# The output projection's moving operand read as two halves in turn

## The chip, the cores and the metric

The kernel runs on one core of one Trainium2 chip. The metric is the device time of one execution in microseconds, the median of the runs shown; lower is better. A run of the kernel before took 280.85 us in the median of three (279.88 to 282.11). Engines are named as the profile names them: PE (TensorE matmul), PEld (TensorE weight load), DVE (VectorE), ACT (ScalarE), POOL (GpSimd), SP (SyncE, which issues all DMAs here).

## The reference

Inputs are q, k and v of shape (8 batches, 8 heads, 576 positions, 64), three weights and a convolution kernel of five taps. Two stages follow each other:

```python
# attention inside chunks of 64 positions, per batch and head
scores = q_c @ k_c.T / 8;  attn = softmax(scores);  out = attn @ v_c
# x: (8, 576, 512), heads side by side
gate = sigmoid(sum over k of conv_w[k] * x shifted by k)      # causal, per batch
val  = x @ w_val                                              # 512 x 512
y    = (gate * val) @ w_out                                   # 512 x 512
```

The last line is the output projection: 4608 rows of 512 numbers times a 512x512 weight.

## The kernel before, in words

The 4608 rows are cut into nine groups g of 512. Attention of a group makes x transposed (features on the 128 partitions, 512 positions along the free dimension, four feature blocks), and the value product and the gate keep this layout. So the output projection of a group, `pr(g, t, c)`, takes as its stationary operand (`lhsT`, loaded by PEld) 128 positions t of the gated values of feature block c, and as its moving operand (`rhs`, streamed by PE) the 512 columns of feature block c of w_out. The result is 128 positions by 512 output features in one PSUM tile `ps`, accumulated over the four blocks c.

Both large products are made in three passes of a four-byte format (fp32r), from a high and a low part of each operand: high x high, high x low, low x high. `pr` issues three matmuls of 128x128 by 128x512; there are 9 x 4 x 4 pieces `P g t c`, so 432 such matmuls. The value product `va` (pieces `V g m c`) is built alike, with the weight as stationary operand and x as the moving one, 512 contiguous words per partition; the first pieces of it, while the weight is not yet split, are plain fp32 matmuls (`vf`, pieces `F`), which appear as two matmul records each.

The parts of w_out live in SBUF as `o_hi` and `o_lo` (lines 168 and 169: 128 partitions x 4 blocks x 512 words). They are made once, early: `lw` loads 128 rows of the weight as 8-byte words by DMA into an `acc` tile, and `w1` to `w7` and `wb` (lines 222 to 256) turn them into the high and low part with elementwise operations of DVE, ACT and POOL, column by column. `bits` on the host (line 604) only reinterprets the array's bytes.

The order of all work is a list written out by hand (`ORDER`, lines 18 to 93); each engine takes its instructions in that order. `SLOTS` fixes which buffer each tile takes. `run` (line 160) issues every instruction, so the profile shows one line, 160, for all; tiles tell them apart: in the profile `ps<-o_hi,...` and `ps<-o_lo,...` are output projection matmuls, `ps<-t,v_hi`, `ps<-t,v_lo` (and the like with t4b, t4a) value matmuls, `ps<-x,t` the plain fp32 ones, `ps<-warm` matmuls on zeros in bf16 that keep PE busy early. `sp` (line 319) is one early step with four fp32r matmuls of the same size whose moving operand is `m[...].unsqueeze(2).broadcast_to([P, 8, D])`: eight words, each repeated 64 times. The finished output tile is copied out of PSUM by ACT or DVE (`oc`) and stored by a DMA (`st`).

## Time and profile before

| what | value |
|---|---|
| runs | 280.85 us median (279.88, 280.85, 282.11) |
| profiled execution, first to last instruction | 278.7 us |
| its whole device time | not shown for this execution; the runs' median is 2.15 us above its span |
| mean granted TensorE clock | 0.998 |
| PE busy | 267.7 us (96%), 3327 instructions |
| PEld / DVE / ACT / POOL busy | 214.4 / 229.0 / 211.2 / 128.0 us |

PE's busy time is the union of its matmuls, whose ends are modelled, so a busy PE need not stream at its best rate. For that, the distance from one matmul's start to the next is the thing to read; the views in order of time give the starts to 0.01 us.

### The profile page before, as it was taken

The numbers are of one execution on the slowest core, as the hardware profiler recorded it, in microseconds if no ns is written. First come the engines' busy times: TensorE is split into PE (matmuls) and PEld (weight loads), VectorE is DVE, ScalarE is ACT, GpSimd is POOL, SyncE is SP. The second block draws the span as 40 slices with busy tenths as digits, with TensorE's granted clock in tenths as the row PEclk, the third lists the DMA queues.
The fourth block names the chain that finished last, engine by engine and source line by source line (L and its number), as shares of the span: only waits on it lengthen the run. The fifth ranks groups of instructions, "written<-read, shape, count | busy, mean of one in ns | idle before, by whom it ended". The sixth has DMA issues, their size and how long they took to land.

```text
span 278.7 us, 7940 instructions
## 1 busy us (share of the span) xinstructions
PE 267.7 (96%) x3327; PEld 214.4 (77%) x3329; DVE 229.0 (82%) x323; ACT 211.2 (76%) x476; POOL 128.0 (46%) x107
## 2 busy tenths in 40 slices
PE   2989999999999999999999999999999999999994
PEld 2555778888788877888888888888888788888883
DVE  0899999999999999999999996999989979732000
ACT  2477899999999996869989769879978774344131
POOL 1357876186315405683770048186432361673300
PEclk9999999999999999999999999999999999999999
DMA  7999998076003630569252407600300240005124
GB/s 278 418 389 332 334 339 303 38 239 217 0 0 97 249 143 9 170 253 292 86 163 106 179 11 276 253 2 2 115 0 5 75 183 8 0 0 202 64 86 177
DMA packets 14291, 42.47 MB, mean 152 GB/s; under 512 B 1712, under 2 KB 1712, under 8 KB 14256
## 3 DMA queue, kind: packets, MB, share of 16 engines
q1 hardware_dynamic: 14256, 41.97, 41.8%
q8 instruction: 26, 0.43, 0.6%
q14 instruction: 9, 0.07, 0.1%
HBM read 32.53 MB, written 9.44 MB: 151 GB/s over the span
## 4 chain that ended last, share of the span: by engine, by line
PE 91%; DVE 4%; DMA 2%; issue 1%; ACT 1%; SPq 0%; DVEq 0%
PE ps L160 80%; PE s L160 6%; PE et L160 6%; DVE t L160 2%; DMA ld<-in_q 2%; DVE rs L160 1%; DVE mx L160 1%; ACT t L160 0%; DVE t2b L160 0%; ACT x L160 0%; ACT t2a L160 0%; SPq L160 0%; ACT mh L160 0%; DVE e_row L160 0%; DVEq L160 0%
## 5 line engine op out<-in xcount | busy, mean ns | idle before, releaser
L160 DVE SCALAR_TENSOR_TENSOR acc<-x,cw,acc 128x516 f32<-128x516 f32 (+1 forms) x144 | 110.9, 807 | 1.7 <-ACT acc L160 0.7
L160 PE MATMUL ps<-t,v_hi 128*128 128x512 f32 x240 | 82.6, 400 | 0.0
L160 PEld LDWEIGHTS ps<-t,v_hi 128*128 128x128 f32 x240 | 45.0, 188 | 10.9 <-issue 0.2
L160 PE MATMUL ps<-t,v_lo 128*128 128x512 f32 x112 | 44.2, 394 | 0.0
L160 PE MATMUL ps<-o_hi,t 128*128 128x512 f32 x96 | 37.4, 401 | 0.0
L160 POOL TENSOR_TENSOR t<-e_row,rs 128x1024 f32<-128x1024 f32 (+1 forms) x13 | 25.6, 1973 | 11.4 <-DVE rs L160 11.1
L160 DVE TENSOR_REDUCE mx<-s 128x16 f32<-128x1024 f32 (+1 forms) x18 | 21.2, 1180 | 7.5 <-PE s L160 7.5
L160 PE MATMUL s<-ld,ld 64*64 64x64 f32 x1120 | 20.5, 222 | 5.5 <-DMA ld<-in_q 5.5
L160 PEld LDWEIGHTS ps<-t,v_lo 128*128 128x128 f32 x112 | 21.1, 188 | 4.8 <-issue 0.2
L160 PEld LDWEIGHTS s<-ld,ld 64*64 64x64 f32 x1120 | 18.5, 137 | 7.5 <-issue 6.9
L160 DVE TENSOR_TENSOR t<-ps,t 128x512 fp32r<-128x512 f32 (+1 forms) x29 | 19.3, 682 | 3.4 <-ACT t L160 3.0
L160 ACT ACTIVATE acc<-x,cw 128x516 f32<-128x516 f32 (+1 forms) x30 | 21.7, 748 | 0.4 <-DVE x L160 0.3
L160 ACT COPY x<-ps 128x512 f32<-128x512 f32 (+3 forms) x41 | 18.3, 492 | 4.8 <-DVE acc L160 2.1
L160 PEld LDWEIGHTS ps<-o_hi,t 128*128 128x128 f32 x96 | 18.0, 188 | 4.3
L160 ACT ACT_TABLE_LOAD x16 | 20.5, 1283 | 1.0 <-PEq L616 0.7
L160 ACT COPY t<-ps 128x512 f32<-128x512 f32 x22 | 13.0, 589 | 10.9 <-PE ps L160 8.7
L160 PE MATMUL ps<-o_lo,t 128*128 128x512 f32 x52 | 20.5, 394 | 0.0
L160 ACT ACTIVATE e_row<-e_row 128x1024 f32<-128x1024 f32 (+1 forms) x14 | 14.0, 1000 | 7.7 <-DVE e_row L160 7.6
L160 ACT ACTIVATE e_row<-s,mx 128x64 f32<-128x64 f32 x64 | 19.0, 357 | 0.1
L160 DVE TENSOR_REDUCE rs<-e_row 128x16 f32<-128x1040 f32 (+1 forms) x15 | 17.2, 1147 | 1.6 <-ACT e_row L160 1.6
L160 ACT CAST t<-ps 128x512 fp32r<-128x512 f32 x28 | 16.1, 597 | 1.7 <-PE ps L160 1.7
L160 PEld LDWEIGHTS ps<-t,ld 64*64 64x64 f32 x832 | 13.3, 135 | 3.8 <-ACT t L160 1.8
(301 smaller groups left out, 601.9 us busy)
## 6 DMA issues: line engine op xcount, KB each, us to landing
ld<-in_k SPq DMA_DIRECT2D x18, 512.0 KB, 5.8
ld<-in_q SPq DMA_DIRECT2D x18, 512.0 KB, 5.3
ld<-in_v SPq DMA_DIRECT2D x18, 512.0 KB, 5.5
out<-t SPq DMA_DIRECT2D x14, 256.0 KB, 2.5
acc<-in_moe_w_val SPq DMA_DIRECT2D x4, 512.0 KB, 8.1
acc<-in_moe_w_out SPq DMA_DIRECT2D x4, 512.0 KB, 6.5
out<-t2j SPq DMA_DIRECT2D x2, 256.0 KB, 4.0
out<-t2g SPq DMA_DIRECT2D x2, 256.0 KB, 3.1
```

The lines of the kernel that those rows point to most:

```text
L160: return tc.keep_in_program_order(fn(*args, **kwargs))
```

## The change

The matmuls of `pr` get a view of the weight in which the 512 words of a partition are taken as two halves of 256 and read alternately: word 0 of the first half, word 0 of the second half (1024 bytes further on), word 1 of the first half, and so on. On the host, the columns of w_out are laid out so that this reading order is the old column order: the even columns fill the first half, the odd ones the second. The output, its layout, the instructions and their order stay as they are.

```diff
+    def in_turn(a):
+        return a.rearrange("p (h n) -> p n h", h=2)
...
         for n, (y, w) in enumerate(((gh, wh), (gh, wl), (gl, wh))):
-            run(E.matmul, o_ps[g, t], lhsT=y[g, c][:, ts], rhs=w["o"][:, c, :], start=(c == 0 and n == 0),
+            run(E.matmul, o_ps[g, t], lhsT=y[g, c][:, ts], rhs=in_turn(w["o"][:, c, :]), start=(c == 0 and n == 0),
                 stop=(c == NH - 1 and n == 2))
...
+    def halves(a):
+        return a.reshape(a.shape[0], -1, 2).transpose(0, 2, 1).reshape(a.shape)
...
-        "moe_w_out": bits(inputs["moe_w_out"]),
+        "moe_w_out": bits(halves(inputs["moe_w_out"])),
```

## Rows read from the trace of the kernel before

**Rows 1.** The page: busy us (share of the span) and instructions per engine.
```profile
PE 267.7 (96%) x3327; PEld 214.4 (77%) x3329; DVE 229.0 (82%) x323; ACT 211.2 (76%) x476; POOL 128.0 (46%) x107
```
**Rows 2.** Busy us (instructions) per stretch and engine, granted clock, DMA.
```profile
40.00:272.00 232.00, 232.00 (x2653) 190.05 (x2652) 197.03 (x275) 183.84 (x430) 105.73 (x80) 1.00 0.34 118
...
40.00:60.00 20.00, 20.00 (x336) 16.49 (x334) 19.93 (x32) 19.87 (x60) 10.26 (x7) 1.00 0.64 228
...
160.00:180.00 20.00, 20.00 (x333) 16.72 (x332) 16.70 (x24) 17.27 (x33) 9.95 (x8) 1.00 0.53 193
...
260.00:270.00 10.00, 10.00 (x45) 8.08 (x44) 0.00 (x0) 1.66 (x3) 0.23 (x1) 1.00 0.21 79
```
**Rows 3.** The chain that ended last, by engine, then its final long piece.
```profile
PE 91%; DVE 4%; DMA 2%; issue 1%; ACT 1%; SPq 0%; DVEq 0%
...
210.99 63.98 PE ps L160 x392
```
**Rows 4.** All waits of PE: who waited for whom, us, times, longest.
```profile
PE s L160 <- DMA ld<-in_q: 5.5, 1, 5.5
PE et L160 <- ACT t L160: 1.1, 2, 0.9
PE ps L160 <- issue: 0.3, 1, 0.3
PE ps L160 <- ACT t L160: 0.2, 1, 0.2
```
**Rows 5.** Stretch 60:279, instructions of `o_hi` alone, then `o_lo` (first count: PE).
```profile
60.00:279.00 219.00, 95.78 (x288) 54.00 (x288) 3.03 (x4) 2.59 (x4) 1.00 0.31 110
...
60.00:279.00 219.00, 56.80 (x144) 27.08 (x144) 3.03 (x4) 1.00 0.31 110
```
**Rows 6.** PE in order of time, output projection: start us, length us, what.
```profile
255.28 0.39 PE L160 MATMUL ps<-o_hi,t2d 128*128 128x512 f32 x1
...
274.57 0.40 PE L160 MATMUL ps<-o_hi,t 128*128 128x512 f32 x1
```
**Rows 7.** The same view, value product.
```profile
32.00 0.63 PE L160 MATMUL ps<-t,v_hi 128*128 128x512 f32 x2
...
34.10 0.40 PE L160 MATMUL ps<-t,v_hi 128*128 128x512 f32 x1
```
**Rows 8.** The same view, bf16 and the `sp` matmuls of repeated words.
```profile
13.74 1.67 PE L160 MATMUL ps<-warm 128*128 128x512 bf16 x7
...
15.47 0.38 PE L160 MATMUL s<-ml,minus 128*128 128x512 f32 x1
15.69 0.38 PE L160 MATMUL s<-mh,minus 128*128 128x512 f32 x1
15.90 0.38 PE L160 MATMUL s<-ml,minus 128*128 128x512 f32 x1
```
**Rows 9.** The same view, plain fp32; then durations min/median/max of those records.
```profile
38.78 1.88 PE L160 MATMUL ps<-x,t 128*128 128x512 f32 x4
...
L160 PE MATMUL ps<-x,t x16: 591/592/697, 19.9 to 40.1; 128*128 128x512 f32 x16
```
**Rows 10.** Durations of the bf16 records of Rows 8, min/median/max.
```profile
L160 PE MATMUL ps<-warm x19: 379/379/634, 7.8 to 82.8; 128*128 128x512 bf16 x19
```
**Rows 11.** Groups by form, ACT: every second word of `acc`, then contiguous words.
```profile
L160 ACT ACTIVATE t<-acc 128x512 uint32<-128x512 uint32 x3 | 2.0, 664 | 0.2 <-DMA acc<-in_moe_w_val 0.2
...
L160 ACT ACTIVATE t<-t 128x512 f32<-128x512 f32 x5 | 3.1, 627 | 0.0
```
**Rows 12.** Weight loads of the output projection, then of `sp`, ns min/median/max.
```profile
L160 PEld LDWEIGHTS ps<-o_hi,t x96: 186/188/192, 73.3 to 274.3; 128*128 128x128 f32 x96
...
L160 PEld LDWEIGHTS s<-mh,minus x2: 189/190/190, 15.0 to 15.5; 128*128 128x128 f32 x2
```
**Rows 13.** The page, DMA issues: count, KB each, us to landing.
```profile
acc<-in_moe_w_out SPq DMA_DIRECT2D x4, 512.0 KB, 6.5
```

## Prediction

> **What bounds the kernel now.** I read the engine totals first: PE is busy for 96% of the span, DVE for 82% [rows 1]. [...] The chain that ended last agrees: 91% of it is PE, and its last long piece is 64 us of matmuls into `ps` without a break [rows 3]. Of PE's waits only the first, 5.5 us for a load, is large; the others come to 1.6 us [rows 4]. So PE's own rate sets the end, and whatever a matmul gains or loses goes to the end, as long as the other engines keep up.

> The rate is read from starts, not from busy time. In the tail 84 output projection matmuls stand between 255.28 and 274.57 us with nothing else on PE [rows 6]: 83 steps in 19.29 us, **232.4 ns** each. The value matmuls, alike in size and format, make nine steps in 2.10 us, 233 ns [rows 7]. Two other rows of the same 512 columns are quicker. Seven bf16 matmuls take 1.67 us, of which the last lasts 0.379 [rows 8, 10]: (1.67 - 0.379) / 6 = **215.2 ns**. The `sp` matmuls, fp32r with a weight load of the same size and length [rows 12], start at 15.47, 15.69 and 15.90 [rows 8]: 215 ns. [...] So neither the format, the weight load (188 ns, under every step [rows 12]) nor the array asks for 232 ns. [...] About 17 ns of each output projection matmul is late delivery of the moving words.

> **The change part by part.** *Host layout and load.* The same four DMAs of 512 KB [rows 13] bring the same bytes; the elementwise splitting does not care which column it handles. Cost: nothing, and nothing here hides anything. *Instructions.* Number, order, waits, weight loads and PSUM writes are the same; nothing is moved past a queue and no wait is added. *Reading order.* The 288 + 144 = 432 matmuls of `o_hi` and `o_lo` [rows 5] read words from two places 1024 bytes apart in alternation. No PE row of the trace shows such a stream, so its price is bounded from both sides.

> Below: the step can't fall under the array's rate, 215.2 ns. The gain is at most 232.4 - 215.2 = 17.2 ns, times 432 = **7.4 us**. [...] If instead the step of today simply doubles, it is 465 ns: +100 us. The one row of a scattered read on another engine is mild: ACT reading every second word took 664 ns against 627 for contiguous ones [rows 11], 6%; on a 232.4 ns step that would be 14 ns, +6 us. It reads one place with gaps, though, not two places.

> I take the lower end. [...]

> *How much of the 7.4 us reaches the end.* The 84 matmuls of the tail (1.4 us) come when DVE has ended and ACT is nearly idle [rows 2]; ACT's copies and the last store follow as before. The other 348 (6.0 us) run beside DVE, which has only 35 us of idle time in the 232 and 0.07 in the 20 from 40 to 60, but 3.3 from 160 to 180 [rows 2]. A PE that runs ahead may there catch up with a subtraction or a gate product that DVE hasn't made. I take 1 us off for that: -6.4 us. The profiled execution's whole time isn't shown; its span is 278.7 us, and 2.15 us lie between it and the median of the runs. I keep these: 278.7 - 6.4 + 2.15 = **274.4 us**.

> **The rivals.** *B, a word at a time (slower).* Place: the moving operand's reads. If words are fetched together with their neighbours, and what was fetched beside the wanted word is lost when the next column asks elsewhere, every column costs a fetch of its own. For it: 17 ns are lost even on contiguous words, so the supply has no slack at one new word per column [rows 6 to 8]. Against it: the gapped read of ACT lost 6% only [rows 11]. It decides as soon as the step exceeds 232.4 ns; PE is full [rows 2], so nothing hides any of it, and every other engine would wait for PE. At 429 ns: 280.85 + 85 = **365.8 us**; at 465 ns 381 us.

> [...]

> *C, no difference.* If supply is limited by bytes alone, or if what was fetched from both places is kept, the step stays at 232.4 ns whatever the order: **280.9 us**. For it: the value and the projection steps agree within 1 ns, though their operands lie in different places [rows 6, 7]. Against it: `sp` reaches 215 ns with the same count of four-byte reads, so it isn't the count alone [rows 8].

> [...]

> *D, the gain is there but another engine takes it back.* The step falls to 215 ns and PE then waits for DVE for all that lies beside it: only the tail's 1.4 us is left, 279.4 us. DVE's 35 idle us speak against it. I count it in C.

> **How the numbers follow.** About 1% (2.8 us) is what a measurement of this kernel can tell from no change. Chances: faster, the step near 215 ns, 0.43; C with D, within 1%, 0.17; B, slower, 0.40, since a supply that already falls short is a bad place to scatter reads, and the quick rows show less demand rather than this order. The likeliest case's own range is 272.5 (the full 7.4 us, and 1 us for the runs' scatter) to 278 us (the gain near 1%). Case B belongs in an 8-in-10 range: it goes up to 368 us, which holds the 429 ns step and all milder ones; left out is most of what lies above it, 465 ns and more.

> **What would show it.** In the changed kernel the distance between starts of `o_hi` and `o_lo` matmuls in the tail decides: near 215 ns is my forecast, 232 is C, 300 or more is B. Value matmuls must stay at 232 to 233 ns in every case; if they move too, something else than the order changed. If the step falls but the time doesn't, PE will show new waits for DVE between 40 and 160 us. I am wrong if scattered four-byte reads lose what adjacent ones share.

## The result, and the profile after

The changed kernel takes **277.13 us** in the median of four runs (276.15 to 277.75) against 280.37 for the kernel before (four runs, 279.65 to 282.11): ratio 0.988, 95% interval 0.984 to 0.991. It is faster by 3.2 us, 1.2%. The forecast was 274.4 us, so about half of the forecast gain came.

First the rate. In order of time on PE in the changed kernel (start us, length us, what), the first and last of the same 84 output projection matmuls as in [rows 6]:

```profile
253.92 0.38 PE L160 MATMUL ps<-o_hi,t2d 128*128 128x512 f32 x1
254.13 0.38 PE L160 MATMUL ps<-o_lo,t2d 128*128 128x512 f32 x1
...
271.83 0.38 PE L160 MATMUL ps<-o_hi,t 128*128 128x512 f32 x1
```

83 steps in 17.91 us: **215.8 ns** a step instead of 232.4. The value product kept its order and its rate; the same view early in the changed kernel:

```profile
32.25 0.63 PE L160 MATMUL ps<-t,v_hi 128*128 128x512 f32 x2
...
34.35 0.40 PE L160 MATMUL ps<-t,v_hi 128*128 128x512 f32 x1
```

Nine steps in 2.10 us, 233 ns, as in [rows 7]. So the 432 steps save 432 x 16.6 = 7.2 us of PE's time. The span fell from 278.7 to 276.0 us, 2.7 us. The rest must have gone into gaps of PE. The page of the changed kernel (busy per engine; then the chain that ended last, by engine):

```profile
PE 263.0 (95%) x3329; PEld 214.7 (78%) x3329; DVE 231.4 (84%) x323; ACT 211.6 (77%) x476; POOL 129.8 (47%) x107
...
DVE 39%; PE 29%; ACT 16%; issue 9%; POOL 4%; DMA 2%; SPq 0%; POOLq 0%; ACTq 0%; DVEq 0%
```

The chain was 91% PE before [rows 3]; now it is 29% PE and 39% DVE. All waits of PE in the changed kernel (us in total, times, longest):

```profile
PE s L160 <- DMA ld<-in_q: 5.5, 1, 5.5
PE et L160 <- ACT t L160: 1.1, 2, 0.9
PE ps L160 <- ACT t L160: 1.1, 2, 0.9
PE et L160 <- POOL t L160: 0.5, 1, 0.5
PE ps L160 <- POOL t2s L160: 0.5, 1, 0.5
PE s L160 <- DVE t L160: 0.4, 1, 0.4
```

Beside [rows 4] there are new waits for pieces that ACT, POOL and DVE make. The largest, in order of time on PE:

```profile
166.56 0.40 PE L160 MATMUL ps<-t,v_lo 128*128 128x512 f32 x1
166.79 0.39 PE L160 MATMUL ps<-t,v_hi 128*128 128x512 f32 x1
168.04 0.50 PE L160 MATMUL ps<-t,v_hi 128*128 128x512 f32 x1 [0.85 <-ACT t L160]
```

The step is 1.25 us where 0.23 were due: 1.0 us lost, though the idle time reads 0.85, since a matmul's record (0.39 us) is longer than the step (0.23). The ACT piece waited for, the copy `t<-ps` at 167.38, stands behind one that waits for DVE: ACT sat idle for 2.06 us until DVE had finished a convolution tap (`acc`). ACT in order of time, in the changed kernel and then the second row as it was before:

```profile
164.23 0.57 ACT L160 CAST t<-ps 128x512 fp32r<-128x512 f32 x1
166.85 0.65 ACT L160 COPY x<-ps 128x256 f32<-128x256 f32 x2 [2.06 <-DVE acc L160]
167.38 0.60 ACT L160 COPY t<-ps 128x512 f32<-128x512 f32 x1
...
166.39 0.65 ACT L160 COPY x<-ps 128x256 f32<-128x256 f32 x2 [2.05 <-DVE acc L160]
```

ACT's wait is not new; it ended 0.46 us later than before. New is that PE arrives early: the matmul ahead starts at 166.79 us against 167.99 before, the waiting one at 168.04 against 168.22. So of a lead of 1.20 us 0.18 was left. Followed back from here, the chain that ended last runs through ACT's copies and then, from 166.8 back to 89.7 us, through DVE and its short issue times alone. From 40 to 168 us DVE had little room (busy us per engine in the order of [rows 2], DVE third; before, then after):

```profile
40.00:168.00 128.00, 128.00 (x1777) 105.47 (x1776) 124.86 (x180) 115.75 (x281) 59.74 (x44) 1.00 0.42 145
...
40.00:168.00 128.00, 126.64 (x1778) 105.70 (x1776) 126.35 (x180) 115.55 (x280) 59.65 (x44) 1.00 0.43 145
```

DVE was idle for 3.1 of these 128 us before and for 1.7 after. Its 180 instructions there also took 1.5 us longer, and this is the taps' doing. All 144 of them, before and after (busy us, mean ns):

```profile
L160 DVE SCALAR_TENSOR_TENSOR acc<-x,cw,acc 128x516 f32<-128x516 f32 (+1 forms) x144 | 110.9, 807 | 1.7 <-ACT acc L160 0.7
...
L160 DVE SCALAR_TENSOR_TENSOR acc<-x,cw,acc 128x516 f32<-128x516 f32 (+1 forms) x144 | 113.3, 824 | 1.5 <-ACT acc L160 0.4
```

Why they took longer is not shown. Taps with no POOL instruction beside them took 747 ns in both kernels (98 and 94 taps); those with POOL busy all along took 914 ns before (17) and 1012 after (19).

Instruction by instruction against the trace of before, the first output projection matmul starts 0.27 us later than before (73.77 against 73.50) and the last one 2.74 us earlier: 3.0 us gained in between, so 7.2 - 3.0 = **4.2 us** were given back there. Fifteen steps that grew by over 60 ns add up to 3.8 us of it. The largest are 1.02 us at 168.04, 0.70 at 122.50 and 0.60 at 247.51, waits for ACT, POOL and POOL. At 168.04 us, 192 of the 432 matmuls had saved 3.2 us, of which 0.45 was left; the loss behind that point is 1.4 us.

### The profile page after: what moved, and what is told of

It reads as the page before. It is cut to its first block, busy times and chain, and to the rows that moved or that the text cites. A ratio compares the mean times of both kernels' runs of the same rounds, so it can differ in the third digit from the quotient of the medians.

```text
span 276.0 us, 7942 instructions
## 1 busy us (share of the span) xinstructions
PE 263.0 (95%) x3329; PEld 214.7 (78%) x3329; DVE 231.4 (84%) x323; ACT 211.6 (77%) x476; POOL 129.8 (47%) x107
## 4 chain that ended last, share of the span: by engine, by line
DVE 39%; PE 29%; ACT 16%; issue 9%; POOL 4%; DMA 2%; SPq 0%; POOLq 0%; ACTq 0%; DVEq 0%
PE ps L160 25%; DVE acc L160 19%; DVE t L160 6%; ACT t L160 4%; DVE mx L160 4%; DVE rs L160 4%; ACT e_row L160 2%; PE s L160 2%; DVE e_row L160 2%; POOL t L160 2%; ACT acc L160 2%; PE et L160 2%; DMA ld<-in_q 2%; ACT x L160 1%; ACT L160 1%
## 5 line engine op out<-in xcount | busy, mean ns | idle before, releaser
L160 DVE SCALAR_TENSOR_TENSOR acc<-x,cw,acc 128x516 f32<-128x516 f32 (+1 forms) x144 | 113.3, 824 | 1.5 <-ACT acc L160 0.4
L160 PE MATMUL ps<-o_hi,t 128*128 128x512 f32 x96 | 35.9, 386 | 0.0
L160 PE MATMUL ps<-o_lo,t 128*128 128x512 f32 x52 | 19.7, 379 | 0.0
L160 DVE TENSOR_REDUCE rs<-e_row 128x16 f32<-128x1040 f32 (+1 forms) x15 | 17.2, 1149 | 1.5 <-ACT e_row L160 1.5
L160 PE MATMUL et<-ident,t 128*128 128x128 f32 x120 | 15.8, 275 | 0.8 <-POOL t L160 0.5
```

The costliest lines, as they stand in the source:

```text
L160: return tc.keep_in_program_order(fn(*args, **kwargs))
```

## The experiments

Two questions: what about the order makes the step 216 ns, and where the other half of the gain went. For the first, seven kernels differ from the changed one in the order in which the words of a weight row are read, each with the host layout that keeps the output's columns in place; each has a single run. Words 0 to 511 are positions in the row, A and B its two halves.

**Every second word.**

```diff
-        return a.rearrange("p (h n) -> p n h", h=2)
+        return a.rearrange("p (n h) -> p h n", h=2)
```

> Only the reading order of the output projection's moving operand differs from the changed kernel (host layout to match): words 0, 2, 4, ... 510, then 1, 3, ... 511. Theory 1 (a neighbourhood of SBUF can't give a new word in every column; the halves help because each is walked at half speed): here one place is walked at double speed, so the step should be above 232 ns, 250 to 430, and the kernel at 288 to 366 us. Theory 2 (only directly adjacent words in successive columns hurt): no two successive words are adjacent, so 216 ns and about 277 us.

Measured: 376.41 us. Tail of the output projection, first and last of the 84 matmuls:

```profile
332.68 0.61 PE L160 MATMUL ps<-o_hi,t2d 128*128 128x512 f32 x1
...
370.22 0.65 PE L160 MATMUL ps<-o_hi,t 128*128 128x512 f32 x1
```

37.54 us / 83 = 452 ns. Reading words that aren't adjacent doesn't help as such; theory 2 falls. The step lies above the 250 to 430 ns of theory 1, too. The run also shows a step between rival B's 429 and 465 ns, only not for the order of the change.

**Every fourth word.**

```diff
-        return a.rearrange("p (h n) -> p n h", h=2)
+        return a.rearrange("p (n h) -> p h n", h=4)
```

> Words 0, 4, 8, ... 508, then 1, 5, ...: each word 16 bytes from the one before. Theory 1: one place walked at four times the speed, 430 ns or more, 365 us or more. Theory 2: 216 ns, about 277 us. A theory 3 (the step depends on how often a 16-byte piece is left after a single word, whatever the order) gives the same as theory 1 here, but would also have slowed the halves.

Measured: 378.23 us, step 461 ns from the same tail (333.81 to 372.05 us). That is within theory 1's "430 ns or more", but four times the speed costs hardly more than double (461 against 452 ns); theory 1 had the direction, not how it grows.

**Halves near each other.**

```diff
-        return a.rearrange("p (h n) -> p n h", h=2)
+        return a.rearrange("p (n h w) -> p n w h", h=2, w=4)
```

> The halves are taken in turn, but near each other: words 0, 4, 1, 5, 2, 6, 3, 7, then 8, 12, 9, 13, ...: a hop of 16 bytes instead of 1024. Theory 1, if the place is a 16-byte piece: two pieces walked at half speed, 216 ns, 277 us. Theory 1, if the place is something wider (the two have to be far apart): 232 ns, 280 us. Theory 2: 216 ns, 277 us.

Measured: 277.46 us. The tail:

```profile
253.62 0.38 PE L160 MATMUL ps<-o_hi,t2d 128*128 128x512 f32 x1
...
271.53 0.38 PE L160 MATMUL ps<-o_hi,t 128*128 128x512 f32 x1
```

215.8 ns, as in the changed kernel. The distance of 1024 bytes is not what helps; 16 bytes do the same.

**Halves in turn by pairs.**

```diff
-        return a.rearrange("p (h n) -> p n h", h=2)
+        return a.rearrange("p (h n w) -> p n h w", h=2, w=2)
```

> The two halves 1024 bytes apart, in turn by pairs: words 0, 1 of the first, 0, 1 of the second, 2, 3 of the first, ... Theory 1 (average speed in each place is half of the old): 216 ns, 277 us. Theory 2 (adjacent words in successive columns hurt): every second step is between adjacent words, so half of the loss is left, about 224 ns, or all of it, 232 ns: 278.5 to 280.5 us.

Measured: 324.48 us. The tail:

```profile
290.64 0.49 PE L160 MATMUL ps<-o_hi,t2d 128*128 128x512 f32 x1
...
318.43 0.50 PE L160 MATMUL ps<-o_hi,t 128*128 128x512 f32 x1
```

335 ns: both theories wrong, and by far. Each half is walked at half speed on average here too, so theory 1 falls. What differs from the changed kernel is what every *second* column reads. That gave theory 4, an inference from the steps measured so far: take every second column by itself and count the words in a row that it reads from one piece of four words (16 bytes); four went with 215.8 ns, two with 232.4, one with 335 to 461.

**Quarters in turn.**

```diff
-        return a.rearrange("p (h n) -> p n h", h=2)
+        return a.rearrange("p (h n) -> p n h", h=4)
```

> Four quarters of 128 words in turn, 512 bytes apart: words 0, 128, 256, 384, 1, 129, ... Theory 1 (each place is walked more slowly than before): 216 ns, 277 us. Theory 4, formed from the runs so far (even and odd columns are fetched as two streams of their own, and each stream is quick as long as it takes several words in a row from one 16-byte piece: 4 in a row 216 ns, 2 in a row 232, 1 in a row 330 to 460): the even columns read words 0, 256, 1, 257, ..., one in a row between two places, as in the pairs run: about 335 ns, 324 us.

Measured: 300.64 us. The tail:

```profile
271.46 0.43 PE L160 MATMUL ps<-o_hi,t2d 128*128 128x512 f32 x1
...
294.64 0.45 PE L160 MATMUL ps<-o_hi,t 128*128 128x512 f32 x1
```

279 ns. Theory 1 (216) is out. Theory 4 had the side but not the size (335): on every second column both orders go back and forth between two pieces, here with four visits a piece (279 ns), in the pairs run with two (335 ns).

**Halves in turn by fours.**

```diff
-        return a.rearrange("p (h n) -> p n h", h=2)
+        return a.rearrange("p (h n w) -> p n h w", h=2, w=4)
```

> The two halves in turn by four words: 0, 1, 2, 3 of the first, 0 to 3 of the second, ... Theory 4: the even columns read 0, 2 of the first, 0, 2 of the second: two in a row from a 16-byte piece, as in the contiguous order, so 232 ns and 280 us; jumps between pieces as such cost nothing. A theory that only far jumps cost (fewer of them than in the pairs run, which took 335 ns): between 232 and 335, about 280 ns, 300 us. Theory 1: 216 ns, 277 us.

Measured: 287.89 us, step 250 ns (261.18 to 281.94 us). Theory 4 said 232: here too every second column reads two words in a row from a piece, as in the contiguous order, but the next piece is far away, and the step is 18 ns longer (250 against 232.4).

**Close by, in one piece.**

```diff
-        return a.rearrange("p (h n) -> p n h", h=2)
+        return a.rearrange("p (n w h) -> p n h w", w=2, h=2)
```

> Words 0, 2, 1, 3, then 4, 6, 5, 7: no two successive columns read adjacent words, but all four come from one 16-byte piece. Theory 4: the even columns read 0, 1, 4, 5, two in a row from a piece: 232 ns, 280 us, like the contiguous order. Theory 2 (adjacent words in successive columns hurt, alternation helps): 216 ns, 277 us.

Measured: 280.05 us. The tail:

```profile
254.83 0.39 PE L160 MATMUL ps<-o_hi,t2d 128*128 128x512 f32 x1
...
274.12 0.40 PE L160 MATMUL ps<-o_hi,t 128*128 128x512 f32 x1
```

232.4 ns, as theory 4 said and theory 2 did not: alternating inside one piece is as slow as the contiguous order. The orders side by side:

| order | even columns read | words in a row from a 16-byte piece | step ns |
|---|---|---|---|
| halves in turn (the change) | A0 A1 A2 A3 | 4 | 215.8 |
| near halves | 0 1 2 3, 8 9 10 11 | 4 | 215.8 |
| contiguous (before) | 0 2, 4 6 | 2 | 232.4 |
| close by | 0 1, 4 5 | 2 | 232.4 |
| halves by fours | A0 A2, B0 B2 | 2, then a far change | 250 |
| quarters in turn | A0, C0, A1, C1 | 1, each piece visited 4 times | 279 |
| halves by pairs | A0, B0, A2, B2 | 1, each piece visited twice | 335 |
| every second | 0, 4, 8 | 1 | 452 |
| every fourth | 0, 8, 16 | 1 | 461 |

**Where the gain went.** The fifth tap of the convolution is left out in both kernels (36 of DVE's 144 tap instructions, so the gate is computed from four taps).

```diff
     def kt_(g, hp, j):
+        if j == TAPS - 1:
+            return
```

In the kernel before:

> The kernel before, with the fifth tap of the convolution left out (36 DVE instructions of about 0.8 us, 29 us of DVE's work). PE was full with or without them, so every theory: 279.5 to 281 us, within 1% of before.

Measured: 280.31 us median, ratio to before 0.999 (0.996 to 1.002). DVE was busy for 203.4 us instead of 229.0, and the time stayed: DVE's load alone did not matter before. In the changed kernel:

> The changed kernel with the same tap left out. Theory G (the missing 4 us of the gain went into waits of PE for pieces that DVE, and what depends on DVE, had not made yet): with DVE relieved the whole 432 x 16.6 ns = 7.2 us shows against the kernel before without this tap: about 273 us. Rival (the gain is lost within PE, between its matmuls, or at the end of the kernel): it stays near 277 us.

Measured: 275.06 us median, ratio to before 0.978 (0.975 to 0.981). Its page, chain by engine:

```profile
PE 87%; DVE 7%; issue 2%; DMA 2%; ACT 1%; POOL 1%; SPq 0%; DVEq 0%
```

PE is the chain again. The time is 2 us above the 273 of theory G and 2 us below the 277 of its rival. Without the tap the order of reading is worth 280.31 - 275.06 = 5.3 us instead of 3.2. Between the first and the last output projection matmul PE gained 6.0 us of the 7.2 (first 0.68 us later, last 274.72 against 269.41); so, going by one profile of each kernel, 3.0 of the 4.2 us given back were DVE's doing, directly or through ACT and POOL. The 0.68 us in front go with one wait of PE that the profile doesn't explain (`issue`); the largest waits of PE in that kernel:

```profile
PE s L160 <- issue: 1.3, 1, 1.3
PE et L160 <- ACT t L160: 1.1, 2, 0.9
PE et L160 <- POOL t L160: 0.4, 1, 0.4
```

**The value product in turn as well.** The moving operands of the value matmuls get the same view; the positions then stand in another order in PSUM, and the read-out puts them right. (Helper views are written out here; the plain fp32 matmuls and the gate product on DVE are changed alike.)

```diff
-            run(E.matmul, v_ps[g, m], ..., rhs=x[g, c // 2][:, c % 2], ...
+            run(E.matmul, v_ps[g, m], ..., rhs=in_turn(x[g, c // 2][:, c % 2]), ...
...
-        run(copy, out=v_sb[g, m], in_=v_ps[g, m])
+        run(copy, out=v_sb[g, m].rearrange("p (h n) -> p h n", h=2), in_=v_ps[g, m].rearrange("p (n h) -> p h n", h=2))
```

> The changed kernel, with the value product's moving operand (x, and the plain fp32 one) also read as two halves in turn; the positions then stand in another order in PSUM, and the copy or gate product that reads them out puts them right by a view of every second word. 408 fp32r matmuls gain 16.6 ns each if the step depends on the reading order alone: 6.8 us less work for PE, value step 216 ns. Theory G: most of it goes into waits for DVE again, 273.5 to 277 us, and DVE becomes the longest part of the chain. If PE were still the bound: 270.3 us. If the read-out of every second word in PSUM is dearer: above 277 us.

Measured: 278.34 us median, ratio to before 0.990 (0.987 to 0.993), above theory G's range and where a dearer read-out would have put it. But the value step is 216 ns (from 32.46 to 33.97 us seven steps in 1.51 us) and the read-out costs no more (ACT's copies `t<-ps`, of values and outputs together, take 591 ns on average in both). PE now waits in more places, and the plain fp32 matmuls got slower. Their four records in order of time, and their durations min/median/max:

```profile
39.18 2.32 PE L160 MATMUL ps<-x,t 128*128 128x512 f32 x4
...
L160 PE MATMUL ps<-x,t x16: 701/704/804, 20.0 to 40.8; 128*128 128x512 f32 x16
```

(2.32 - 0.704) / 3 = 539 ns against (1.88 - 0.592) / 3 = 429 in [rows 9]: a slowdown whose cause is not shown and that speaks against simply alternating everything.

**The same, but the first group left contiguous.**

```diff
+    def x_turn(g, a):
+        return in_turn(a) if g else a
...
```

> As the run with the value product read in turn, but the first group (with all plain fp32 matmuls, whose records took 540 ns instead of 429 when read in turn, 16 x 0.11 = 1.8 us) keeps the contiguous order. 384 value matmuls save 16.6 ns each, 6.4 us of PE's work. Theory G (PE now runs ahead of DVE): nearly none of it reaches the end, 275.5 to 277.5 us, with DVE the longest part of the chain. Rival (the value product's order has a cost of its own, in the read-out): 278 us or more, as in that run. If PE were still the bound: 270.7 us.

Measured: 277.84 us median, ratio to before 0.991 (0.988 to 0.994): no better than the changed kernel. That is 0.3 us above theory G's range and just below its rival's 278; the chain and the waits decide for G. The plain fp32 records are back at 592 ns in the median. Its chain by engine, and its largest waits of PE behind the first load:

```profile
DVE 51%; ACT 19%; PE 12%; issue 10%; POOL 5%; DMA 1%; SPq 0%; POOLq 0%; ACTq 0%; DVEq 0%
```

```profile
PE et L160 <- POOL t L160: 2.8, 3, 1.0
PE ps L160 <- ACT t L160: 2.0, 4, 1.3
```

PE is only 12% of the chain: 6.4 us less work for PE brought nothing.

**The same, without the fifth tap.**

> The same kernel with the fifth tap of the convolution left out. Theory G: with 29 us of DVE's work gone both reading orders show, 280.3 - 7.2 - 6.4 = 266.7 us at best, 268 to 270 with about the waits that the changed kernel without this tap kept. Rival (the value product's order brings nothing): 275 us.

Measured: 270.44 us median, ratio to before 0.964 (0.960 to 0.969). With DVE relieved the two reading orders together bring 280.31 - 270.44 = 9.9 of 13.6 us (the two kernels ran on different chips, where the kernel before took 280.65 and 279.94 us). The work saved on PE was real in the run before this one; it had no place to go.

## Why the prediction was right and wrong

*What bounds.* Right for the kernel before, and the reading of 17 ns of late delivery was right too: with another order the same matmul runs at 215.8 ns. The sign, the forecast step (near 215) and the unmoved value step (232 to 233) are all as forecast.

*Reading order.* The term of 7.4 us measured 7.2. The reason put on record for it with the first runs, theory 1 (each half walked at half the speed), is wrong: pairs walk each half as slowly, quarters walk each place more slowly still, and they take 335 and 279 ns. So the number was right by luck. In theory 4's count, which is inferred, the halves let every second column read four words in a row from one piece (215.8 ns), the contiguous order two (232.4).

*How much reaches the end.* This is the step that was mis-sized: 1 us was taken off, and 4.2 us were. Of DVE's 35 idle us from 40 to 272 only 3.1 lie ahead of 168 us; the other 32 lie behind, when two thirds of DVE's work is done. Ahead of 168 us PE was to gain 3.2 us and kept 0.45. DVE's taps took 2.4 us longer besides, which the prediction didn't foresee. It expected new waits for DVE between 40 and 160 us; of the three largest losses one lies there, and PE's own waits are for ACT and POOL, with DVE behind those at 122.50 and 168.04. Idle time of another engine is no slack unless it lies before the piece that PE will wait for. Rival D, all of the gain before the tail taken back, was as near the truth as the forecast: 277.1 lies about midway between 274.4 and 279.4. That the time fell into the forecast's own 272.5 to 278 us is owed to the width of that range.

*Rival B* was given 0.40 on the ground that a short supply is a bad place to scatter reads. For another order its numbers were met: every second word takes 452 ns, between its 429 and 465. For this order they were not: the next column asks elsewhere every time, and the step is 215.8 ns; none of the nine orders has a shorter one. The 429 ns behind its 365.8 us ((429 - 232.4) x 432 is the 85 us more) is the step of a plain fp32 record [rows 9]; no run shows it for an output projection matmul, whose slow orders took 250, 279, 335, 452 and 461 ns.

*Rival C* falls: the same bytes in nine orders take seven different steps from 216 to 461 ns.

## What to carry to other kernels

When a matmul stream runs without gaps on a full engine, compare its start-to-start step with rows of the same width and another operand (here 232.4 against 215 ns) before looking for waits; the order of the moving words can be a lever, as for these four-byte operands, and a host layout made it free here. Check orders on the chip one by one, since others were up to 2.1 times as slow as the good one (461 against 215.8 ns). And before counting a gain on a full engine, ask for each engine beside it whether it is idle just ahead of the pieces that the faster engine will want; a sum of idle time says nothing on that.

## What the runs showed of the hardware

- An fp32r matmul of 128x512 whose moving words are contiguous steps at 232.4 ns, 17 ns above the best order measured; with the two halves in turn it steps at 215.8 ns, with every second word in sequence at 452 ns. In the tail, contiguous steps vary from 226 to 239 ns, those of the halves in turn from 215 to 216.
- Plain fp32 behaves the other way: 429 ns a record with contiguous words, 539 with halves in turn (the four records at 38.78 and 39.18 us).
- ACT's and DVE's read-out of every second word in PSUM took no longer than a contiguous one (128x512: 591 ns on average for ACT's copies `t<-ps` in both kernels; 685 against 691 ns for DVE's gate products `t2q<-ps,t`).
